# Sliding-window attention: products with the values for two query blocks at once, and one copy of both every second slot

## The chip, the cores and the metric

The kernel runs on one core of one Trainium2 chip. The metric is the device time of one execution in microseconds (us); lower is better. The engines are named as in the profile: PE is TensorE's matmul part, PEld its weight loads, DVE is VectorE, ACT is ScalarE, POOL is GpSimd, SP is SyncE, whose queue issues the transfers.

## What is computed

A block with 2048 tokens of width 512. The input is normalised, goes through attention with 32 heads of width 16 and a window of 256 keys, and through a gated feed-forward part of width 1792:

```python
xn = layernorm(x)                                   # 2048 x 512
q, k, v = split(xn @ wqkv)                          # 32 heads, 16 wide
scores = q @ k.T * 16 ** -0.5                       # per head
mask = (i - j >= 0) & (i - j < 256)
s = (softmax(where(mask, scores, -1e9)) @ v) @ wo
g = silu(gelu(layernorm(xn) @ w1 + b1) @ w2 + b2)
out = x + s * g                                     # all in float32
```

With blocks of 128 tokens, the window of a query block reaches over its own key block and the two before it.

## The kernel before

The program has one core's instructions in an order written by hand: a list of fillers and planned steps gives each step its slot, and all engines but SP keep that order. There are two long stages. Up to about 449 us attention runs, with the projections and a part of the feed-forward's first product as fillers; after that comes the rest of the feed-forward, the output projection and the gate.

Attention is cut into 128 slots: 8 groups of four heads (`n`) times 16 blocks of 128 tokens. Slot `t` does, in PE's order:

1. `prob_block(..., 1)`: scores of key block `t` against up to three query blocks (384 columns) for two of the four heads into the bank pair `stb`, in two matmuls side by side, one in the upper 64 rows of the array, one in the lower. ACT takes the exponential into `pt`, and POOL clears what lies outside the window in the first and the last 128 columns (`affine_select`).
2. `max_block`: for query block `t + 12` (`LEAD = 12`), the scores against the window's keys, to get the row maxima. The two newer key blocks go to `xy` (four matmuls of 256 columns), the oldest to `zo[:, :, 0:256]` (four of 128). DVE puts the part of `zo` that lies in the window into `xy` (`copy_predicated`) and takes the maximum (`tensor_reduce`). The maxima become an extra row of the queries through a small transfer, so that the exponential needs no separate subtraction.
3. `fill_in(t, 0)`: fillers, mostly projections of later heads into the banks `fb`. `tandem` runs two of them side by side on half the array's rows each; in the middle of their span (`mid`) the two banks change rows.
4. `prob_block(..., 0)`: as 1., for the other two heads; then `fill_in(t, 1)`.
5. `pv_step` for query block `t - 1`: the products with the values. `vt` holds the values with a column of ones (17 columns a head), so that the denominators come along. For each of the up to three key blocks and each of the four heads there is one product of 128 columns, with the head's 17 output rows at partition 32 times its number, so that the four heads' products lie side by side in the array's columns. They add up in `otb`, 128 columns of the bank `zo[:, 1]`, whose first 256 columns belong to `max_block`.
6. ACT copies `otb` to a quarter of `oraw`; every fourth slot SP sends `oraw` to memory (`oT_d`).

```python
otb = zo[:, 1, 256:384]
```

`xy`, `zo`, `stb` and `otb` exist once, so each is written again only after its readers are done. Readers and writers of one bank are kept apart by waits: the first `zo<-qk` matmul of `max_block` waits for ACT's copy of `otb`, and the first product of `pv_step` for DVE's `copy_predicated`. A plain float32 product is two matmuls in the instruction stream, which the counts of the profile show.

In the profile nearly all instructions carry line L42, that of a helper which issues them; they are told apart by their tiles: `zo<-pt,vt` the products with the values, `oraw<-zo` the copy, `zo<-qk` and `xy<-qk` the scores for the maxima, `stb<-qk` those for the exponential, `fb<-...` the fillers.

Of the kernel before, what the change touches and what calls it, by code (L numbers as in the profile page):

```python
# [9 lines left out]
F32 = mybir.dt.float32  # L10
# [7 lines left out]
S, D, H, DH, WIN, F = 2048, 512, 32, 16, 256, 1792  # L18
P = 128
# [30 lines left out]
def mixer_kernel(ctx, tc, x, wqk, wv, wo, w1, b1, w2, b2, out):  # L50


    nc = SimpleNamespace(**{name: Ordered(tc, name) for name in ("tensor", "vector", "scalar", "gpsimd", "sync")})
# [4 lines left out]
    small = ctx.enter_context(tc.tile_pool(name="small", bufs=3))  # L58
# [72 lines left out]
    def run(steps):  # L131
        for step in steps:
            step()
# [13 lines left out]
    def open_slot(i):  # L147
        slots.append(bigp.tile([P, 2, 2, S], F32R, tag=f"qk{i}", name=f"qk{i}"))
# [13 lines left out]

    xy = psum.tile([P, 2, 512], F32, name="xy")
    zo = psum.tile([P, 2, 512], F32, name="zo")
    otb = zo[:, 1, 256:384]
    fb = [psum.tile([P, 512], F32, name=f"fb{i}") for i in range(2)]
    early = ExitStack()
    ps_st = early.enter_context(tc.tile_pool(name="ps_st", bufs=2, space=PSUM))
# [8 lines left out]
    vt = vp.tile([P, NKB, 16, DH + 1], F32, name="vt")  # L177
# [210 lines left out]
    def pair_h(f):  # L388
# [11 lines left out]
                behind(t, nc.sync.dma_start, h_d[f - 6], raw)  # L400
        return 3 * KT, mm, finish

    def tandem(t0, t1, one, two, mid=None, back=None):

        n = one[0]
        lo, hi = slice(0, 64), slice(64, P)
        mid = mid or max(1, (t0 + t1 + 1) // 2)
        most = n // 4  # L410

        def places(slots, last):

            last = min(most, n // (len(slots) + 1)) if last else 0
            cuts = [(n - last) * k // len(slots) for k in range(len(slots) + 1)]
            out = []
            for t, a, b in zip(slots, cuts, cuts[1:]):
                ahead = min(b - a, max(most, (b - a + 1) // 2))
                out += [(t, 0)] * ahead + [(t, 1)] * (b - a - ahead)
            return out + [(t1, 0)] * last  # L420

        first, second = places(range(t0, mid), False), places(range(back or mid, t1), True)
        for phase, where in enumerate((first, second)):
            for i in range(n):
                flags = dict(start=(phase == 0 and i == 0), stop=(phase == 1 and i == n - 1), skip_group_check=True)
                def unit(i=i, phase=phase, flags=flags):
                    (two if phase == 0 else one)[1](fb[1 - phase], i, hi, **flags)
                    (one if phase == 0 else two)[1](fb[phase], i, lo, **flags)
                fills.setdefault(where[i], []).append((unit, ()))
        fills[t1, 0].append((one[2], (fb[0], t1, nc.scalar.copy)))  # L430
        fills[t1, 0].append((two[2], (fb[1], t1, nc.vector.tensor_copy)))
# [12 lines left out]

    mts = {}

    def max_block(n, qb):

        slot = slots[n % 2]
        if qb % 4 == 0:  # L450
            mts[n, qb // 4] = small.tile([P, 2, 2, 4], F32, tag="mt", name=f"mt_{n}_{qb}")
        lo = max(qb - 1, 0)
        off = 128 * (lo + 1 - qb)

        def scores(p, a, first):
            r = slice(64 * a, 64 * a + 64)
            out, keys = ((zo[:, a, P * p: P * (p + 1)], slice(P * (qb - 2), P * (qb - 1))) if first else
                         (xy[:, a, 256 * p + off: 256 * (p + 1)], slice(P * lo, P * (qb + 1))))
            nc.tensor.matmul(out, slot[r, 0, p, P * qb: P * (qb + 1)], slot[r, 1, p, keys], start=True, stop=True)

        for p, a, first in ((0, 1, False), (0, 0, False), (1, 1, False), (1, 0, False),
                            (0, 1, True), (0, 0, True), (1, 1, True), (1, 0, True)):
            if qb >= 2 or not first:
                scores(p, a, first)
        four = xy.rearrange("q a (p k) -> q a p k", p=2)
        nc.vector.copy_predicated(four[:, :, :, 128:256], mask,
                                  neg if qb < 2 else zo[:, :, 0:256].rearrange("q a (p k) -> q a p k", p=2))
        nc.vector.tensor_reduce(out=mts[n, qb // 4][:, :, :, qb % 4],
                                in_=four[:, :, :, off:256],
                                axis=AX.X, op=ALU.max, negate=True)  # L470
# [15 lines left out]
    pts = {}  # L486

    def prob_block(n, kb, p):
        slot = slots[n % 2]
        w = min(384, S - P * kb)  # L490
        pt = pp.tile([P, 2, 384], F32, tag="pt", name=f"pt_{n}_{kb}_{p}")
        both = xy if p and 16 * n + kb + LEAD >= 16 * NQ else stb[0]
        for a in (1, 0):
            r = slice(64 * a, 64 * a + 64)
            nc.tensor.matmul(both[:, a, 0:w], slot[r, 1, p, P * kb: P * (kb + 1)],
                             slot[r, 0, p, P * kb: P * kb + w], start=True, stop=True)
        nc.scalar.activation(pt[:, :, 0:w], both[:, :, 0:w], AF.Exp, scale=DH ** -0.5)
        nc.gpsimd.affine_select(out=pt[:, :, 0:P], in_=pt[:, :, 0:P], pattern=[[0, 2], [1, P]],
                                compare_op=ALU.is_ge, fill=0.0, base=0, channel_multiplier=-1)
        if w == 384:  # L500
            nc.gpsimd.affine_select(out=pt[:, :, 256:384], in_=pt[:, :, 256:384],
                                    pattern=[[0, 2], [-1, P]], compare_op=ALU.is_gt, fill=0.0,
                                    base=0, channel_multiplier=1)
        pts[(n, kb, p)] = pt


    outs = {}

    def pv_step(n, qb):

        lo = max(qb - 2, 0)
        for kb in range(lo, qb + 1):
            for j in range(4):
                nc.tensor.matmul(otb[32 * j: 32 * j + DH + 1], vt[:, kb, (4 * n + j) % 16],
                                 pts[n, kb, j // 2][:, j % 2, P * (qb - kb): P * (qb - kb + 1)],
                                 start=(kb == lo), stop=(kb == qb),
                                 skip_group_check=True, tile_position=(0, 32 * j))
        if qb % 4 == 0:
            outs[0] = sgp.tile([P, 512], F32, tag="or", name=f"oraw_{n}_{qb}", bufs=2)
        nc.scalar.copy(outs[0][:, P * (qb % 4): P * (qb % 4 + 1)], otb)  # L520
        if qb % 4 == 3:
            (at if n or qb > 7 else behind)(16 * n + qb + 2, nc.sync.dma_start, oT_d[n // 2, n % 2::2, :, P * (qb - 3): P * (qb + 1)], outs[0])

# [81 lines left out]
    def at(t, fn, *args):  # L605
        plan.setdefault(t, []).append((fn, args))
# [33 lines left out]
    n, raw = raws["qk"]  # L640
# [27 lines left out]
    for place, todo in spread([job_qk(1, 0), job_qk(1, 1)], [(t, k) for t in range(-2, 3) for k in range(2)]).items():  # L668
        fills.setdefault(place, []).extend(todo)
    soon = {}  # L670
    tandem(3, 8, pair_qk(1, 2), pair_qk(1, 3))
    for n, spans in enumerate((((9, 14), (15, 19)), ((20, 24), (25, 30)), ((31, 35), (36, 41)), ((42, 47), (48, 53, 51)),
                               ((75, 79), (80, 84)), ((85, 90), (93, 98))), 2):
# [68 lines left out]
    def fill_in(t, half):  # L742
        now[:] = t, half
        run(delayed.pop((t, half), ()))
        for fn, args in fills.get((t, half), ()):
            fn(*args)

    end = 16 * NQ
    for t in range(-16, end + 1):
        m = t + LEAD  # L750
        if t == -5:
            open_slot(1)
            for k in range(4):
                at(-4 + k, clear_part, k)
        if 0 <= t < end:
            if t == 0:
                early.close()
                stb.append(attn.enter_context(tc.tile_pool(name="ps_s2", bufs=1, space=PSUM)).tile(
                    [P, 2, 512], F32, name="stb"))
            prob_block(t // 16, t % 16, 1)  # L760
        if t >= 0 and m < end:
            max_block(m // 16, m % 16)
        fill_in(t, 0)
        for fn, args in plan.get(t, []):
            fn(*args)
        if 4 <= m < LEAD:
            max_block(0, m)
        if 0 <= t < end:
            prob_block(t // 16, t % 16, 0)
        fill_in(t, 1)  # L770
        if 0 <= m < 4:
            max_block(0, m)
        if t >= 1:
            pv_step((t - 1) // 16, (t - 1) % 16)
        run(lns.get(t, ()))
        if 0 <= m < end and m % 4 == 3:
            max_rows(m // 16, m % 16 // 4, t)
        for fn, args in ends.get(t, []):
            fn(*args)
# [20 lines left out]
    for f in range(6, NF, 2):  # L800
        t = gp.tile([P, 2, 512], F32, tag="ohl", name=f"hr_{f}", bufs=4)
# [403 lines left out]
```

## Time and profile before

| | us |
|---|---|
| median of 3 runs | 773.82 |
| lowest and highest of them | 773.26, 775.31 |
| the profiled execution, its own time | 776.17 |
| its span, first to last instruction | 774.5 |

| engine | busy us | share | instructions |
|---|---|---|---|
| PE | 747.9 | 97% | 7428 |
| PEld | 583.5 | 75% | 7428 |
| DVE | 533.4 | 69% | 865 |
| ACT | 435.3 | 56% | 724 |
| POOL | 281.5 | 36% | 567 |

The granted TensorE clock is 0.998 of full speed over the span. A matmul's length in the profile includes its way through the array, so matmuls that overlap fill PE's row, and a PE that is busy 97% of the time isn't at its peak: what a stretch of matmuls costs is read from the starts of one and of the next. The chain of work that ended last is followed back from the last instruction; an engine's share of it is time that it alone held up the end, as far as the profile shows. A releaser named in a wait is the one that came last.

### The profile page before, as it was taken

To read this page: it belongs to the slowest core of one execution; us is meant where nothing else is said; L and a number is where in the kernel's file an instruction comes from. 1 tells how busy PE (TensorE), PEld (TensorE's weight loads), DVE (VectorE), ACT (ScalarE), POOL (GpSimd) and SP (SyncE) were. 2 spreads that over 40 slices of the span, in tenths; PEclk is the share of its full clock that TensorE was granted. 3 is DMA by queue.
4 is the path that set the end of the run, shared out by engine and by line. 5 is a ranking of instruction groups with operands and counts; after the bars stand their busy time and mean duration, and the time that the engine had idled before them with its cause. 6 is when DMAs were issued, how large, how long until landed. Compare 5 with 4: busy or idle time off the path is not lost.

```text
span 774.5 us, 18774 instructions
## 1 busy us (share of the span) xinstructions
PE 747.9 (97%) x7428; PEld 583.5 (75%) x7428; DVE 533.4 (69%) x865; ACT 435.3 (56%) x724; POOL 281.5 (36%) x567
## 2 busy tenths in 40 slices
PE   9889999999999999999999999999999999999997
PEld 8777666676768887676676678888778778888886
DVE  7886777777777778887874447763657475676473
ACT  5536776767676666777877755444544444442001
POOL 6111666757565554766766800030101100000102
PEclk9999999999999999999999999999999999999999
DMA  7612445655446863455744283541102213243531
GB/s 258 204 44 52 106 110 121 172 114 139 111 92 201 256 213 98 107 150 138 186 128 151 61 287 118 180 150 56 68 28 98 92 61 101 84 137 135 177 96 54
DMA packets 56951, 99.40 MB, mean 128 GB/s; under 512 B 11104, under 2 KB 11360, under 8 KB 56864
## 3 DMA queue, kind: packets, MB, share of 16 engines
q1 hardware_dynamic: 56864, 98.21, 43.4%
q8 instruction: 58, 0.95, 0.5%
q14 instruction: 29, 0.24, 0.1%
HBM read 51.39 MB, written 29.62 MB: 105 GB/s over the span
## 4 chain that ended last, share of the span: by engine, by line
PE 80%; DVE 9%; ACT 6%; issue 3%; POOL 2%; DMA 1%; SPq 0%; DVEq 0%; ACTq 0%; POOLq 0%
PE acc L42 18%; PE fb L42 17%; PE zo L42 13%; PE stb L42 8%; PE p L42 7%; PE s L42 6%; PE xy L42 5%; PE h L42 5%; ACT pt L42 3%; PE pv L42 1%; DVE xnT L42 1%; DVE xy L42 1%; DVE mt L42 1%; POOL pt L42 1%; DVE bnA L42 1%
## 5 line engine op out<-in xcount | busy, mean ns | idle before, releaser
L42 POOL TENSOR_SCALAR_AFFINE_SELECT pt<-pt 128x256 f32<-128x256 f32 x480 | 193.6, 428 | 158.8 <-ACT pt L42 156.5
L42 ACT ACTIVATE pt<-stb 128x768 f32<-128x768 f32 (+1 forms) x244 | 188.7, 773 | 55.3 <-PE stb L42 46.2
L42 DVE TENSOR_REDUCE mt<-xy 128x4 f32<-128x1024 f32 (+1 forms) x128 | 152.6, 1192 | 4.4
L42 PE MATMUL acc<-w,gh 128*128 128x512 f32 x432 | 133.3, 390 | 0.0
L42 DVE COPY_PREDICATED xy<-upper,zo 128x512 f32<-128x512 int32 x112 | 77.5, 692 | 69.4 <-PE zo L42 67.5
L42 PE MATMUL fb<-xnT,wqb 64*128 64x512 f32 (+1 forms) x684 | 115.4, 405 | 0.5 <-DVE xnT L42 0.5
L42 PE MATMUL zo<-pt,vt 128*17 128x128 f32 x2880 | 103.9, 275 | 2.2 <-DVE xy L42 1.6
L42 PE MATMUL stb<-qk 64*128 64x384 f32 (+1 forms) x488 | 96.6, 391 | 7.2 <-ACT pt L42 5.8
L42 POOL TENSOR_TENSOR xo<-xo,gated 128x512 f32<-128x512 f32 x15 | 20.2, 1350 | 220.9 <-DVE gated L42 217.3
L42 PEld LDWEIGHTS zo<-pt,vt 128*17 128x17 f32 x2880 | 67.4, 97 | 39.7 <-issue 18.0
L42 PEld LDWEIGHTS acc<-w,gh 128*128 128x128 f32 x432 | 80.8, 188 | 16.6
L42 PEld LDWEIGHTS stb<-qk 64*128 64x128 f32 x488 | 45.5, 183 | 52.1 <-ACT pt L42 41.0
L42 PE MATMUL acc<-w,gl 128*128 128x512 f32 x216 | 84.2, 390 | 0.0
L42 PEld LDWEIGHTS fb<-xnT,wqb 64*128 64x128 f32 (+1 forms) x684 | 63.4, 186 | 7.3 <-DVE xnT L42 0.6
L42 PE MATMUL xy<-qk 64*128 64x256 f32 (+2 forms) x536 | 61.7, 304 | 5.5 <-DVE mt L42 4.7
L42 ACT COPY oraw<-zo 128x128 f32<-128x128 f32 x128 | 34.2, 267 | 40.5 <-PE zo L42 36.4
L42 PEld LDWEIGHTS xy<-qk 64*128 64x128 f32 x536 | 43.8, 185 | 17.2 <-DVE mt L42 9.8
L42 PEld LDWEIGHTS acc<-w,gl 128*128 128x128 f32 x216 | 40.5, 188 | 8.7 <-DVE gl L42 0.3
L42 ACT ACTIVATE gated<-acc 128x512 f32<-128x512 f32 x16 | 8.7, 596 | 64.0 <-DVE acc L42 64.0
L42 PE MATMUL s<-wos,ohl 128*128 128x512 f32 (+1 forms) x204 | 44.7, 377 | 0.0
L42 DVE TENSOR_TENSOR gl<-g,gh 128x512 fp32r<-128x512 f32 x38 | 28.1, 740 | 20.6 <-ACT gh L42 19.3
L42 PEld LDWEIGHTS s<-wos,ohl 128*128 128x128 f32 x204 | 36.6, 188 | 7.0
(182 smaller groups left out, 1172.3 us busy)
## 6 DMA issues: line engine op xcount, KB each, us to landing
qk<-sh SPq DMA_DIRECT2D x128, 128.0 KB
qk<-pjr SPq DMA_DIRECT2D x64, 128.0 KB
oT_d<-oraw SPq DMA_DIRECT2D x32, 256.0 KB
w_d<-in_w_dram SPq DMA_DIRECT2D x14, 512.0 KB
x<-in_x_dram SPq DMA_DIRECT2D x16, 256.0 KB
or<-oT_d SPq DMA_DIRECT2D x16, 256.0 KB
w<-rden_d SPq DMA_DIRECT2D x16, 256.0 KB
xo<-in_x_dram SPq DMA_DIRECT2D x16, 256.0 KB
```

The source lines that it names most:

```text
L42: r = issue(*args, **kwargs)
```

## The change

`pv_step` now works on pairs of query blocks. `otb` is 256 columns, both blocks of a pair. In the slot of the even block the two key blocks before the pair are taken: the newer of them for both query blocks in one product of 256 columns, the older for the even block alone, 128 columns. In the slot of the odd block come the pair's own two key blocks: the even one for both query blocks (256 columns), the odd one for the odd block (128). A slot has 8 products in place of 12, with the same number of columns in all. The sums stay open in `otb` from the even slot to the odd one, and ACT copies 256 columns after the odd block.

Two things go with it. `max_block`'s `zo<-qk` matmuls of the bank with `otb` come between the two halves of an open sum; there they no longer carry the flag that marks the whole bank as fresh (`amid`). And where a slot with an even block comes just before the middle of a `tandem`, ACT reads one column of `otb` (`seen`), so that the order of the work around that middle stays fixed by a wait, as it was by the copy; there are 14 of these.

```diff
-    otb = zo[:, 1, 256:384]
+    otb = zo[:, 1, 256:512]
...
+    turns = set()
...
         mid = mid or max(1, (t0 + t1 + 1) // 2)
+        turns.add(mid - 1)
...
-    def max_block(n, qb):
+    def max_block(n, qb, amid=False):
...
-            nc.tensor.matmul(out, slot[r, 0, p, P * qb: P * (qb + 1)], slot[r, 1, p, keys], start=True, stop=True)
+            nc.tensor.matmul(out, slot[r, 0, p, P * qb: P * (qb + 1)], slot[r, 1, p, keys],
+                             start=not (amid and first and a), stop=True, skip_group_check=amid)
...
     def pv_step(n, qb):
 
-        lo = max(qb - 2, 0)
-        for kb in range(lo, qb + 1):
+
+        even = qb - qb % 2
+        blocks = ((1,) if qb else (0,)) if even == 0 else (even, qb) if qb % 2 else (even - 1, even - 2)
+        for kb in blocks:
+            first, last = max(even, kb), min(even + 1, kb + 2)
             for j in range(4):
-                nc.tensor.matmul(otb[32 * j: 32 * j + DH + 1], vt[:, kb, (4 * n + j) % 16],
-                                 pts[n, kb, j // 2][:, j % 2, P * (qb - kb): P * (qb - kb + 1)],
-                                 start=(kb == lo), stop=(kb == qb),
+                nc.tensor.matmul(otb[32 * j: 32 * j + DH + 1, P * (first - even): P * (last + 1 - even)],
+                                 vt[:, kb, (4 * n + j) % 16],
+                                 pts[n, kb, j // 2][:, j % 2, P * (first - kb): P * (last + 1 - kb)],
+                                 start=(kb == max(even - 1, 0)), stop=(kb >= even),
                                  skip_group_check=True, tile_position=(0, 32 * j))
-        if qb % 4 == 0:
+        if qb % 2 == 0:
+            if 16 * n + qb + 1 in turns:
+                nc.scalar.copy(small.tile([P, 1], F32, tag="seen", name=f"seen_{n}_{qb}"), otb[:, 0:1])
+            return
+        if qb % 4 == 1:
             outs[0] = sgp.tile([P, 512], F32, tag="or", name=f"oraw_{n}_{qb}", bufs=2)
-        nc.scalar.copy(outs[0][:, P * (qb % 4): P * (qb % 4 + 1)], otb)
+        nc.scalar.copy(outs[0][:, 128 * (qb % 4 - 1): 128 * (qb % 4 + 1)], otb)
...
-            max_block(m // 16, m % 16)
+            max_block(m // 16, m % 16, t >= 2 and t % 2 == 0)
```

## The prediction

> **What bounds the kernel now.** I read first the page's busy time and the chain of work that ended last, then the stages.
>
> ```profile
> span 774.5 us, 18774 instructions
> PE 747.9 (97%) x7428; PEld 583.5 (75%) x7428; DVE 533.4 (69%) x865; ACT 435.3 (56%) x724; POOL 281.5 (36%) x567
> ...
> PE 80%; DVE 9%; ACT 6%; issue 3%; POOL 2%; DMA 1%; SPq 0%; DVEq 0%; ACTq 0%; POOLq 0%
> PE acc L42 18%; PE fb L42 17%; PE zo L42 13%; PE stb L42 8%; PE p L42 7%; PE s L42 6%; PE xy L42 5%; PE h L42 5%; ACT pt L42 3%; PE pv L42 1%; DVE xnT L42 1%; DVE xy L42 1%; DVE mt L42 1%; POOL pt L42 1%; DVE bnA L42 1%
> ```
>
> TensorE (PE) is busy 97% and holds 80% of the chain; zo, where the values' products land, has 13% of it. The change touches only the slots. The first values' product starts at 77.7 us, the last score block for the maxima is done near 418, the last copy of the values at 449.3, so I cut there in the view by stretches of time (columns: stretch, length, busy us and instructions of each engine).
>
> ```profile
> 77.70:418.00 340.30, 330.16 (x5055) 241.88 (x5054) 264.29 (x364) 242.28 (x418) 215.03 (x467) 1.00 0.54 143
> 418.00:449.30 31.30, 30.80 (x469) 21.82 (x468) 12.04 (x22) 23.91 (x42) 20.63 (x46) 1.00 0.39 118
> 449.30:774.50 325.20, 316.88 (x1422) 260.32 (x1422) 196.25 (x354) 126.70 (x210) 26.38 (x20) 1.00 0.34 111
> ```
>
> In the first stretch PE is busy 330 of 340 us, ScalarE (ACT) 242. What the change takes off ACT is thus worth nothing by itself; what it does to PE's order of work counts. The last 325 us don't change.
>
> The groups by form, for what is removed:
>
> ```profile
> L42 PE MATMUL zo<-pt,vt 128*17 128x128 f32 x2880 | 103.9, 275 | 2.2 <-DVE xy L42 1.6
> L42 PEld LDWEIGHTS zo<-pt,vt 128*17 128x17 f32 x2880 | 67.4, 97 | 39.7 <-issue 18.0 <-DVE xy L42 16.7 <-POOL pt L42 1.5
> ...
> L42 ACT COPY oraw<-zo 128x128 f32<-128x128 f32 x128 | 34.2, 267 | 40.5 <-PE zo L42 36.4 <-DVE mt L42 2.8 <-DMA w_d<-in_w_dram 0.3
> ...
> L42 ACT COPY pjr<-fb 128x512 f32<-128x512 f32 x15 | 8.8, 586 | 6.1 <-PE fb L42 4.4 <-PE stb L42 1.7
> ```
>
> Then one slot in order of time (start, length, operation):
>
> ```profile
> 300.70 0.45 PE L42 MATMUL stb<-qk 64*128 64x384 f32 x2
> 300.81 0.37 PEld L42 LDWEIGHTS xy<-qk 64*128 64x128 f32 x4
> 300.84 0.27 ACT L42 COPY oraw<-zo 128x128 f32<-128x128 f32 x1 [0.69 <-PE zo L42]
> 300.99 0.40 PE L42 MATMUL xy<-qk 64*128 64x256 f32 x4
> ...
> 301.16 0.30 PEld L42 LDWEIGHTS zo<-qk 64*128 64x128 f32 x4
> 301.22 0.38 PE L42 MATMUL zo<-qk 64*128 64x128 f32 x4
> 301.27 0.81 ACT L42 ACTIVATE pt<-stb 128x768 f32<-128x768 f32 x1 [0.16 <-PE stb L42]
> ...
> 301.44 0.91 PE L42 MATMUL fb<-xnT,wqb 64*128 64x512 f32 x6
> ...
> 302.18 0.40 PE L42 MATMUL stb<-qk 64*128 64x384 f32 x2
> ...
> 302.42 0.39 PE L42 MATMUL fb<-xnT,wqb 64*128 64x512 f32 x2
> ...
> 302.63 0.81 ACT L42 ACTIVATE pt<-stb 128x768 f32<-128x768 f32 x1 [0.54 <-PE stb L42]
> ...
> 302.74 0.85 PE L42 MATMUL zo<-pt,vt 128*17 128x128 f32 x24
> ...
> 303.52 0.38 PE L42 MATMUL stb<-qk 64*128 64x256 f32 x2
> ```
>
> A slot lasts 2.8 us (300.70 to 303.52) and the values' 24 matmuls take 0.78 of it (302.74 to 303.52). The copy of the values runs at the start of the next slot, 300.84 to 301.11. The weight load of zo<-qk, the oldest block's scores for the maxima, starts at 301.16, 0.05 after it. The built program has a wait of that load for ACT in 100 of 112 places (zo and the values share a bank).
>
> **The change, part by part.**
>
> *Fewer, longer products.* A logical product is two matmuls. 1440 become 960, 2880 matmuls 1920; an even slot and an odd slot each stream 256+128 columns per head in place of three times 128. The columns are the same, so only what a matmul costs beside its columns is saved.
>
> ```profile
> 124.31 0.40 PE L42 MATMUL fb<-xnT,wqb 64*128 64x512 f32 x2
> ...
> 124.63 0.30 PE L42 MATMUL zo<-pt,vt 128*17 128x128 f32 x4
> ```
>
> Four heads run side by side: the first four of this block last 0.30, one alone 0.275, so they start within 0.025. In the block of 24 above, 0.85 less 0.275 leaves 0.575 between the first and the last start; less that 0.025, 0.55 for five rounds of four, 0.11 a round. Is any of it not columns? Pairs of xy<-qk (256 columns) go by in 0.115 (300.99 to 301.22, two pairs), pairs of fb (512 columns) in 0.25 (301.44 to 302.18, three): proportional, with no fixed part. I take 3 ns a round, hardly more than zero: 720 rounds become 480, 240 x 0.003 = -0.7 us. Ends: 0, and -6.0 if every round paid the 0.025 of its starts.
>
> The Trainium skill has a rule here: TensorEngine Tiling, Instruction Overhead, gives every matmul about 60 cycles beside its columns. By an estimate from that figure and the 2.4 GHz in the Trainium skill's TensorE: Matmul & The Clock Gate, What's actually happening, 240 rounds would give back 240 x 25 ns = 6.0 us; by that rule the sum below would be 5.3 us lower, and the pairs of 256 and 512 columns speak against it.
>
> *One copy every second slot.* From 128 columns in 267 ns to 512 in 586, a column is 0.83 ns, so 256 take 0.373: 64 such copies are 23.9 us, and the 14 new one-column copies at 0.16 make 2.2, against 34.2: ACT saves 8 us. Off the path: in the slot above the exponential starts at 301.27, 0.12 after its scores' end at 301.15, and a copy that ended at 301.22 would still be ahead of it.
>
> What is on the path is the load of zo<-qk behind the copy. After an odd block it waits 0.107 longer, and behind it on PE stand the fillers, the second score block and the values. After an even block it waits for nothing or for a one-column copy. Both prices need to know where that load is the last:
>
> ```profile
> 81.30 0.27 ACT L42 COPY oraw<-zo 128x128 f32<-128x128 f32 x1
> ...
> 81.61 0.30 PEld L42 LDWEIGHTS zo<-qk 64*128 64x128 f32 x4
> ...
> 293.97 0.27 ACT L42 COPY oraw<-zo 128x128 f32<-128x128 f32 x1
> ...
> 294.13 0.44 PE L42 MATMUL stb<-qk 64*128 64x384 f32 x2 [0.39 <-ACT pt L42]
> ...
> 294.65 0.34 PE L42 MATMUL zo<-qk 64*128 64x128 f32 x4
> ...
> 294.83 0.44 PE L42 MATMUL fb<-xnT,wqb 64*128 64x512 f32 x2
> ...
> 409.13 0.27 ACT L42 COPY oraw<-zo 128x128 f32<-128x128 f32 x1 [0.69 <-PE zo L42]
> ...
> 409.44 0.30 PEld L42 LDWEIGHTS zo<-qk 64*128 64x128 f32 x4
> ```
>
> The first and last after an odd block start 0.04 after the copy ends. I read all 100 such pairs: the load is held by the copy in 33 of 50 after an odd block and 33 of 50 after an even one. Where the copy was long done, as at 293.97, zo<-qk to the fillers takes 294.65 to 294.83, 0.18; where it holds, 301.22 to 301.44, 0.22. So an even place gives 0.04 (six of them 0.1): -1.7 us. An odd place is already held, so it takes the 0.107 in full, a few of the 33 less: +3.2. Ends: nothing given back, and 50 odd places, +5.4.
>
> In four of the odd places the next slot waits for an exponential held up by a cast that asks nothing of PE, and the delay is lost in that wait: -0.4.
>
> *A second wait ahead of the values.* In the built program the block's first load waits for VectorE (DVE) alone in 93 slots; after the change for DVE and GpSimd (POOL), which costs an instruction more on PE's queue. Cover: PE drains when it changes its tiling. The block at 124.63 had two waits before and starts 0.32 after its filler (124.31), as the one with a single wait does (302.42 to 302.74). Where the cover ends:
>
> ```profile
> 107.40 0.19 PEld L42 LDWEIGHTS stb<-qk 64*128 64x128 f32 x2 [0.21 <-ACT pt L42]
> ...
> 107.65 0.33 PEld L42 LDWEIGHTS xy<-qk 64*128 64x128 f32 x4
> ...
> 317.35 0.67 DVE L42 COPY_PREDICATED xy<-upper,zo 128x512 f32<-128x512 int32 x1
> ...
> 318.08 0.24 PEld L42 LDWEIGHTS zo<-pt,vt 128*17 128x17 f32 x12 [0.95 <-DVE xy L42]
> ```
>
> Where DVE is last, as at 318.02, the cover is gone: there are 16 such starts, 0.06 behind DVE's end. Price of a wait instruction: at 107.40 two of them stand between two loads 0.25 apart that without them are 0.11 apart (300.70, 300.81), so 0.07 each. 16 x 0.075 = +1.2; ends 0 and, in all 93, +7.0.
>
> *Fewer waits on ACT.* 98 exponentials had two or three waits, 56 have; with them one starts 0.12 after its scores (301.15 to 301.27), without 0.05 (302.58 to 302.63). PE asks for that only where it waits for ACT, the second line of this list of waits (us in total, times, longest):
>
> ```profile
> PEld xy L42 <- DVE mt L42: 9.8, 20, 1.7
> ...
> PE stb L42 <- ACT pt L42: 5.8, 15, 1.0
> ```
>
> Half of 15 places, 0.08 each, cut to -0.3; ends 0 and, if half of that wait went, -2.9.
>
> *At no cost.* The larger clearing of zo (once, while x is still loading; below the 0.27 of a copy of as many columns if that cover were gone), the flag that leaves the bank's marks, the order of key blocks (an odd slot's newest block is still second to last by time, 0.43 in place of 0.44 into the block; an even one no longer needs it), the stores of the values (issued 0.107 later, read after 449).
>
> Sum: -0.7 + 3.2 - 1.7 - 0.4 + 1.2 - 0.3 = +1.3 us. The profiled execution took 776.17 (774.5 of span), 2.35 over the median of 773.82, so 777.5 there and 775.1 in the median, +0.17%. A difference below 0.3%, 2.3 us, counts as none.
>
> **The rivals.**
>
> *The gain of the even slots is not had* (chance 0.20). The load of xy waits for DVE's maximum in 20 places, 9.8 us (first line of the waits); where DVE decides, zo<-qk 0.04 earlier helps only if DVE's copy starts earlier too. Without the 1.7 and the absorbed 0.4: +3.4, 777.2, slower. It decides once DVE's ring and not PE sets the slot; for it speaks DVE's 264 us in the stretch, against it PE's 330.
>
> *The second wait ahead of the values isn't covered* (0.13): 93 x 0.075 = 7.0 in place of 1.2, so 780.9, slower. It decides once DVE ends less than some 0.13 us (0.06 and the 0.07 of a wait) before most blocks start. For it speaks the load's wait for DVE (16.7 us in the group above), against it the start at 124.63.
>
> *ACT's relief reaches PE* (0.14). The 8 us off ACT shorten the late exponentials, half of the 5.8 goes, and PE's waits soak up half of the 3.2: 775.1 - 2.6 - 1.6 = 770.9, faster. Against it: in a late slot, as at 294.13, PE comes with the scores after the copy began, and the copy ends (294.24) before the scores do (294.57).
>
> *Time goes by the matmul, not the column* (0.03): 16 in place of 24 would take a third of 0.575, 0.19 in each of 120 slots, 23 us in place of 0.7: 773.8 + 1.3 + 0.7 - 23 = 753. Against it pairs of 512 columns that take twice those of 256. The Trainium skill's Instruction Overhead points this way, by less.
>
> That the products aren't wider is excluded: the built program has 960 of them, half of 256 columns.
>
> **How the numbers follow.** My forecast, no difference beyond 0.3%, has 0.50, its own range 771.5 to 776.1. Slower: 0.20+0.13 = 0.33. Faster: 0.14+0.03 = 0.17. The predicted time is 775.1. The range runs from 770.9, ACT's relief, to 779.5, most of the uncovered wait; outside are the 753 and part of 780.9 and of the rivals' tails.
>
> **What would show it.** Right: values' blocks last as long as before for both slots (0.78 to the next stb), the copy near 0.37, zo<-qk to fillers some 0.1 later after odd blocks and 0.04 shorter after even ones, 340 us of the first stretch within 2. Wrong: a block that shrinks with its count of matmuls; a start of the values more than 0.33 after the filler in many slots; PE's wait for ACT falling from 5.8 to under 3.

## The result: 0.56% slower, and the loss lies where no changed line is at work

The changed kernel takes 779.54 us (median of 6 runs, 777.50 to 780.35) against 774.57 (773.26 to 776.72) for the kernel before in the same session: a ratio of 1.0056, 95% interval 1.0034 to 1.0078 (ratios here and below are taken over all executions and are not quotients of the two medians, which would be 1.0064 here). The profiled execution took 780.27, with a span of 778.6. Executions of one kernel differ by up to 3.5 us, and the traces show 2.5 of it ahead of the slots (the first product with the values starts at 77.74 us in the kernel before and at 75.25 in the experiment e3 below), so stages are compared by their own lengths.

The head of the page of the changed kernel, then its view by stretches of time, cut where the same work begins and ends (its last copy of the values starts 0.55 us earlier):

```profile
span 778.6 us, 16794 instructions
PE 753.0 (97%) x6468; PEld 560.6 (72%) x6468; DVE 532.5 (68%) x865; ACT 426.7 (55%) x674; POOL 280.8 (36%) x567
77.70:418.00 340.30, 330.59 (x4201) 221.44 (x4202) 263.49 (x365) 234.30 (x373) 214.99 (x467) 1.00 0.55 143
418.00:448.75 30.75, 30.48 (x363) 18.92 (x362) 11.56 (x21) 23.16 (x38) 20.16 (x45) 1.00 0.38 116
448.75:778.60 329.85, 321.99 (x1422) 260.89 (x1422) 196.62 (x354) 126.77 (x210) 26.28 (x20) 1.00 0.35 110
```

TensorE executes 960 matmuls fewer and is busy 5.1 us longer (747.9 to 753.0). In the slots nothing is lost; the last stretch, where no line of the diff is at work, goes from 325.2 us to 329.85 with the same 1422 matmuls. That is the whole loss. Where in it? The groups by form, first of the kernel before, then of the changed one:

```profile
L42 PE MATMUL acc<-w,gh 128*128 128x512 f32 x432 | 133.3, 390 | 0.0
L42 PE MATMUL acc<-w,gl 128*128 128x512 f32 x216 | 84.2, 390 | 0.0
L42 PE MATMUL s<-wos,ohl 128*128 128x512 f32 x180 | 41.8, 390 | 0.0
L42 PE MATMUL h<-xnT 128*128 128x512 f32 x112 | 32.3, 389 | 0.0
L42 PEld LDWEIGHTS acc<-w,gh 128*128 128x128 f32 x432 | 80.8, 188 | 16.6
```

```profile
L42 PE MATMUL acc<-w,gh 128*128 128x512 f32 x432 | 136.5, 397 | 0.0
L42 PE MATMUL acc<-w,gl 128*128 128x512 f32 x216 | 85.6, 396 | 0.0
L42 PE MATMUL s<-wos,ohl 128*128 128x512 f32 x180 | 41.9, 391 | 0.0
L42 PE MATMUL h<-xnT 128*128 128x512 f32 x112 | 32.4, 390 | 0.0
L42 PEld LDWEIGHTS acc<-w,gh 128*128 128x128 f32 x432 | 81.0, 188 | 19.2
```

Only acc, the second product of the feed-forward part (`project`), is clearly slower (s and h by 1 ns): 397 ns in place of 390, with no idle time before it and with loads of the same 188 ns. From one start to the next the median goes from 227 to 234 ns, in every chunk and with the granted clock at 1.00: 648 x 7 ns = 4.5 us. The timelines show it as three matmuls in 0.68 us before (first fence, gl to gl) and 0.71 after:

```profile
467.02 0.39 PE L42 MATMUL acc<-w,gl 128*128 128x512 f32 x1
467.25 0.62 PE L42 MATMUL acc<-w,gh 128*128 128x512 f32 x2
467.70 0.39 PE L42 MATMUL acc<-w,gl 128*128 128x512 f32 x1
```

```profile
466.56 0.40 PE L42 MATMUL acc<-w,gl 128*128 128x512 f32 x1
466.80 0.63 PE L42 MATMUL acc<-w,gh 128*128 128x512 f32 x2
467.27 0.40 PE L42 MATMUL acc<-w,gl 128*128 128x512 f32 x1
```

One group of the changed kernel was spared. The first 24 matmuls of acc load their weights from g_first, not from gh and gl:

```profile
L42 PE MATMUL acc<-w,g_first 128*128 128x512 f32 x24 | 5.7, 395 | 0.7 <-ACT hf L42 0.7
453.29 4.48 PE L42 MATMUL acc<-w,g_first 128*128 128x512 f32 x19
```

19 of them in 4.48 us: less the last one's 0.39, 18 steps of 227 ns. Same operation, same moving w2, same chunk; only the tile that the weights come from differs. g_first lies in the pool bigp. In the built program gh and gl lie in a pool that stands behind the pool small, and the diff gives small one more tag, `seen`: three buffers of one column, each rounded up to 32 bytes a partition. So everything behind it lies 96 bytes higher: gh from byte 193280 (755 x 256) to 193376. w2, at 83200 (325 x 256), and g_first stay.

### The profile page after: what moved, and what is told of

Same layout as the page of the kernel before. It is cut to its first block, busy times and chain, and to the rows that moved or that the text cites. A ratio compares the mean times of both kernels' runs of the same rounds, so it can differ in the third digit from the quotient of the medians.

```text
span 778.6 us, 16794 instructions
## 1 busy us (share of the span) xinstructions
PE 753.0 (97%) x6468; PEld 560.6 (72%) x6468; DVE 532.5 (68%) x865; ACT 426.7 (55%) x674; POOL 280.8 (36%) x567
## 4 chain that ended last, share of the span: by engine, by line
PE 82%; DVE 8%; ACT 5%; issue 2%; POOL 2%; DVEq 0%; ACTq 0%
PE acc L42 19%; PE fb L42 17%; PE zo L42 13%; PE stb L42 8%; PE p L42 7%; PE h L42 6%; PE s L42 6%; PE xy L42 5%; ACT pt L42 3%; POOL pt L42 2%; DVE xy L42 1%; PE pv L42 1%; DVE mt L42 1%; DVE xnT L42 1%; DVE bnA L42 1%
## 5 line engine op out<-in xcount | busy, mean ns | idle before, releaser
L42 PE MATMUL acc<-w,gh 128*128 128x512 f32 x432 | 136.5, 397 | 0.0
L42 PE MATMUL zo<-pt,vt 128*17 128x128 f32 (+1 forms) x1920 | 103.1, 329 | 2.6 <-DVE xy L42 1.1
L42 PEld LDWEIGHTS zo<-pt,vt 128*17 128x17 f32 x1920 | 44.1, 96 | 61.1 <-issue 20.6
L42 PE MATMUL zo<-qk 64*128 64x128 f32 x448 | 40.6, 258 | 0.0
```

Source lines behind the costliest of these rows:

```text
L42: r = issue(*args, **kwargs)
```

## The experiments

**Is it the placement? (e1)** The kernel before, plus nothing but the tag:

```diff
     def pv_step(n, qb):
+        if n == qb == 0:
+            small.tile([P, 1], F32, tag="seen", name="pad")
         lo = max(qb - 2, 0)
```

> The kernel before, with one thing of the change alone: the tag 'seen' in the pool small is opened (three buffers of 32 bytes a partition, never written or read), so that every tile of a pool behind it, gh and gl among them, lies 96 bytes higher, as in the changed kernel; no instruction is added or moved. Placement theory (a load of gh or gl that lies 96 bytes off the moving w2 disturbs the product that runs beside it): acc goes from 227 to 234 ns a matmul, 648 x 7 ns = 4.5 us, so ratio 1.006 (778.5 to 780) and the attention stage as before within 0.5 us. Rival, the loss comes from the changed order of the values (what they leave behind on the queues or in the clock): 1.000, acc at 227.

778.87 us against 775.62, ratio 1.0050 (1.0036 to 1.0064). Not one instruction is added, and acc has the changed kernel's rows to the digit:

```profile
L42 PE MATMUL acc<-w,gh 128*128 128x512 f32 x432 | 136.5, 397 | 0.0
L42 PE MATMUL acc<-w,gl 128*128 128x512 f32 x216 | 85.6, 396 | 0.0
```

From the first to the last start of a values' block this kernel takes 370.12 us, the kernel before 370.61. The loss is one of placement; the rival, the order of the values, is out.

**The address of gh and gl, or their distance from w2? (e2)** The kernel before with 96 bytes ahead of everything:

```diff
+    const.tile([P, 24], F32, name="pad")
     ident = const.tile([P, P], F32, name="ident")
```

> The kernel before with 96 unused bytes ahead of the very first constant, so that every tile of the kernel's own, w2 and gh and gl alike, lies 96 bytes higher and no two of them stand otherwise to each other. If what counts is the distance between the loaded and the moving operand: acc at 227, ratio 1.000. If what counts is the address of the loaded operand by itself: acc at 234, and h, p and s as well perhaps, ratio 1.006 or more.

775.67, ratio 0.9996 (0.9986 to 1.0007). gh and gl lie at the very addresses of the changed kernel, and w2 96 bytes higher too:

```profile
L42 PE MATMUL acc<-w,gh 128*128 128x512 f32 x432 | 133.3, 390 | 0.0
L42 PE MATMUL acc<-w,gl 128*128 128x512 f32 x216 | 84.2, 390 | 0.0
```

So the address of the loaded operand by itself doesn't count; the distance between loaded and moving operand does.

**Does it hold for another pair? (e4)** s<-wos,ohl had been spared, since both its tiles moved by the same 96. Here only wos, its moving operand, is moved, in the kernel before:

```diff
+    cp.tile([P, 24], F32, name="pad")
     wos = cp.tile([P, 2, 4, 512], F32R, name="wos")
```

> The kernel before with 96 unused bytes ahead of wos alone. gh, gl, w2 and ohl stay. Distance theory: acc at 227, but s<-wos,ohl, which lay at 227 in both kernels, goes to 234 (204 matmuls x 7 ns = 1.4 us, ratio 1.0018). If it is something of gh and gl or of their pool alone: s at 227, ratio 1.000.

```profile
L42 PE MATMUL s<-wos,ohl 128*128 128x512 f32 x180 | 43.0, 396 | 0.0
L42 PE MATMUL acc<-w,gh 128*128 128x512 f32 x432 | 133.4, 390 | 0.0
```

s goes from 226.8 to 233.6 ns a step (390 to 396 in the group), acc stays. The time, 776.00, ratio 1.001 (1.0000 to 1.0020), agrees with the 1.4 us that this makes, though its interval starts at no change: the rows decide here, not the time.

**The change without the displacement (e3, e10).** First the one-column copies go into a tag that exists:

```diff
-  nc.scalar.copy(small.tile([P, 1], F32, tag="seen", name=f"seen_{n}_{qb}"), otb[:, 0:1])
+  nc.scalar.copy(small.tile([P, 1], F32, tag="ve1", name=f"seen_{n}_{qb}"), otb[:, 0:1])
```

> The changed kernel, with the 14 one-column copies written to the existing tag ve1 in place of a tag of their own; all tiles then lie where they lay before. Placement theory: acc back at 227 ns, the 4.5 us gone, and what the change does to the attention stage is left: 0.5 us faster than before, ratio 0.999 (773.5 to 774.5). Rival, order of the values: ratio stays at 1.006 and acc at 234. The sum of the prediction, +1.3, gives 1.0017.

775.10, ratio 0.9992 (0.9983 to 1.0002); acc back at 227. Then the tag stays, with buffers of 256 bytes, which displaces all behind it by 768:

```diff
-  nc.scalar.copy(small.tile([P, 1], F32, tag="seen", name=f"seen_{n}_{qb}"), otb[:, 0:1])
+  nc.scalar.copy(small.tile([P, 64], F32, tag="seen", name=f"seen_{n}_{qb}")[:, 0:1], otb[:, 0:1])
```

> The changed kernel with one number changed: the buffers of the tag 'seen' are 256 bytes a partition each in place of 4 (rounded up to 32), so that all behind it lies 768 bytes higher than before, and not 96. If only the distance within 256 bytes counts: acc and s at 227, ratio as with the tag ve1, 0.998 to 1.000. If any displacement of gh and gl from where they lay disturbs: 1.005.

```profile
L42 PE MATMUL acc<-w,gh 128*128 128x512 f32 x432 | 133.3, 390 | 0.0
L42 PE MATMUL acc<-w,gl 128*128 128x512 f32 x216 | 84.2, 390 | 0.0
```

775.25, ratio 0.9997 (0.9984 to 1.0010). A number in one allocation, 1 column or 64, decides 0.5% of the kernel. What the change itself is worth is thus no difference that these runs can tell.

**Which distances disturb? (e7, e8)** The kernel before with unused bytes ahead of gh, gl and wos, so that one run tries three distances. One diff for both; e7 has 8, 8 and 32 columns of 4 bytes, e8 32, 8 and 16 (each pad also moves what stands behind it):

```diff
+    cp.tile([P, 32], F32, name="pad")
     wos = cp.tile([P, 2, 4, 512], F32R, name="wos")
...
+        if not pads:
+            gp.tile([P, 8], F32, tag="pa", name="pa", bufs=1)
         gh = gp.tile([P, 512], F32R, tag="gh", name=f"gh_{c}_{f}")
+        if not pads:
+            gp.tile([P, 8], F32, tag="pb", name="pb", bufs=1)
+        pads.append(1)
         gl = gp.tile([P, 512], F32R, tag="gl", name=f"gl_{c}_{f}")
```

> The kernel before with unused bytes ahead of gh (32), of gl (32 more, so 64) and of wos (192 in all); w2 and ohl stay. Any distance that is no multiple of 256 bytes disturbs: acc before gh, acc before gl and s all near 234 ns a matmul. A rule by 64 bytes: only gh (32) is disturbed, gl (64) and s (192) stay at 227.

> As the run with 32, 64 and 192 bytes, with 128 ahead of gh, 160 of gl and 224 of wos. A rule by 128 bytes: gh at 227, gl (32 over 128) and s (32 short of 256) at 234. A rule by 256 bytes: all three at 234. A rule by 64: as by 128 here.

One execution each, 779.75 and 780.60; acc and s:

```profile
L42 PE MATMUL acc<-w,gh 128*128 128x512 f32 x432 | 135.2, 394 | 0.0
L42 PE MATMUL s<-wos,ohl 128*128 128x512 f32 x180 | 43.0, 395 | 0.0
```

```profile
L42 PE MATMUL acc<-w,gh 128*128 128x512 f32 x432 | 136.1, 396 | 0.0
L42 PE MATMUL s<-wos,ohl 128*128 128x512 f32 x180 | 43.0, 396 | 0.0
```

By the matmul beside which the displaced tile is loaded (mean, start to next start; 226.4 to 227.3 undisturbed): gh behind gh at 32 bytes 230.4, at 128 230.1; gl at 64 232.6, at 160 236.8; s with wos at 192 and at 224 233.3 both. No rule by 64 or by 128 bytes: of the distances tried only multiples of 256 were free, the others cost 3 to 10 ns a matmul in these rows.

How the price depends on the distance stays open, and the distance isn't all of it. With gh at 128, the step from gl to gh takes 233.5 where that from gh to gh takes 230.1, with the same moving tile: the place in the sequence counts too. And with wos at 224 the loaded tile lies 32 behind the moving one modulo 256, as with gh at 32, yet the steps take 233.3 and 230.4. Nor is it shown that only the load beside a matmul counts. A matmul of h, whose own tiles are not displaced, takes 228.4 (96 bytes, changed kernel), 235.0 (32, e7) and 232.6 (128, e8) in place of 226.8 when a displaced gh is loaded beside it (ten steps each). But a matmul of acc with displaced weights, beside which a tile of h is loaded that is not displaced, takes 230.3, 239.0 and 229.4 in place of 226.6 as well (seven steps each). So part of the disturbance reaches steps whose next load isn't displaced.

**Is the hold at the odd places on the path? (e6, e5, e9)** All three start from e3. In e6 the copy of the values is made in two, so that it ends later:

```diff
-        nc.scalar.copy(outs[0][:, 128 * (qb % 4 - 1): 128 * (qb % 4 + 1)], otb)
+        for h in range(2):
+            nc.scalar.copy(outs[0][:, 128 * (qb % 4 - 1 + h): 128 * (qb % 4 + h)], otb[:, 128 * h: 128 * h + 128])
```

> The changed kernel with tiles where they lay before, and the copy of 256 columns made as two of 128 (2 x 0.267 in place of 0.373), so that the load of zo<-qk is held 0.16 longer after every odd block. If each held place is on the path: 33 x 0.16 = +5.3 us, ratio about 1.006 beside the 0.9992 of the kernel it is made from. If such delays are lost in later waits: +2 or less, ratio 1.002 at most.

776.86, ratio 1.0023 (1.0012 to 1.0035). I had the size wrong: two copies overlap, and take 0.43 together where one takes 0.37:

```profile
301.96 0.43 ACT L42 COPY oraw<-zo 128x128 f32<-128x128 f32 x2 [0.68 <-PE zo L42]
```

So the load is held 0.06 longer, not 0.16. The odd places grow by 0.034 on average, 50 x 0.034 = 1.7 us, and the values from first to last start by 1.46 (370.05 to 371.51): most of a longer hold does reach the end. That gives the price of a longer hold, not that a shorter one would be a gain. For that e5 issues a pair of fillers ahead of the held load, in 41 places:

```diff
+            if first and ahead:
+                ahead[0][0](*ahead.pop(0)[1])
             if qb >= 2 or not first:
                 scores(p, a, first)
...
-            max_block(m // 16, m % 16, t >= 2 and t % 2 == 0)
+            todo = fills.get((t, 0), [])
+            ahead = [todo.pop(0)] if t > 2 and t % 2 and t - 1 not in turns and m % 16 > 1 and todo and todo[0][0].__name__ == "unit" else []
+            max_block(m // 16, m % 16, t >= 2 and t % 2 == 0, ahead)
```

> The changed kernel with tiles where they lay before (the 14 one-column copies in ve1), and in 41 of the slots that follow an odd block one pair of fb matmuls (0.25 us) is issued between the scores of xy and those of zo, so that the load of zo<-qk no longer stands waiting for the copy of 256 columns. If that wait is on the path, as the prediction priced it (0.107 longer, +3.2 in 33 places): some 0.1 us less in each held place, 3 to 4 us, ratio 0.994 to 0.996. If the time is given back further on, since zo now ends 0.12 later for VectorE: ratio 0.998 to 1.001.

778.60, ratio 1.0044 (1.0027 to 1.0061): both expectations missed, the cover costs. zo comes 0.21 later after the second pair of xy (0.147 to 0.358 on average), and VectorE, which needs zo, and then xy, which needs VectorE's maximum, come later with it. The list of waits, of e3 and of e5:

```profile
PEld xy L42 <- DVE mt L42: 10.1, 22, 1.7
```

```profile
PEld xy L42 <- DVE mt L42: 13.2, 36, 1.7
```

22 such waits become 36, and the values take 373.45 us in place of 370.05. In e9 the values lie in the other bank of zo:

```diff
-    otb = zo[:, 1, 256:512]
+    otb = zo[:, 0, 256:512]
...
-                             start=not (amid and first and a), stop=True, skip_group_check=amid)
+                             start=not (amid and first and not a), stop=True, skip_group_check=amid)
```

> The changed kernel with tiles where they lay before, and the 256 columns of the values in the other bank of zo (that of a=0 in place of a=1). The first of the two side-by-side zo products (a=1) then has no bank in common with the copy; only the second waits for it. If a held place costs by the wait at its load: the load of a=1 goes ahead, some 0.05 of the 0.1 is covered in each of 33 odd places, 1 to 2 us, ratio 0.997 to 0.998. If the end of zo, for which VectorE waits, is what decides: it comes as late as before, ratio 0.999.

775.34, ratio 1.0003 (0.9992 to 1.0013). It tells the two theories apart no further: the first load of zo<-qk is held in 29 of 50 odd places as in e3, so the wait hangs on the tile zo, not on the bank, and nothing had been taken away.

No version was faster than the kernel before by a difference that could be measured; e3 came nearest.

## Why the prediction was right or wrong

The predicted time was 775.1 with no difference as the likeliest case; it came out slower, 779.54, 0.04 past the end of the range (779.5), and for the reason of none of the rivals. By the ratio it is 773.82 x 1.0056 = 778.2 on the base from which the prediction started, inside the range; that is luck, since this end was priced for waits that aren't covered, and those did not come.

**The step that failed** is "The last 325 us don't change." I went by the instructions, of which none in that stretch changes, and didn't ask where their operands lie. The same hole is in "At no cost": the one-column copies do cost ScalarE no more than priced (14 of 159 ns), but they needed a place, and that moved gh and gl. It is worth +4.5 us; without it (e3, e10) the kernel is within 0.1% of the one before, as the likeliest case had it.

**The terms within the slots**, from the traces of four kernels with the old values and three with the new, slot by slot (the same slot agrees to about 5 ns among kernels of one kind):

- *Fewer, longer products*, -0.7: a block goes from 0.780 to 0.775, over 127 blocks -0.6. Two rounds fewer a block are worth 5 ns, so 2.5 a round. The 25 a round that the prediction estimated from the 60 cycles of the Trainium skill's TensorEngine Tiling (Array Packing), Instruction Overhead, did not come.
- *Odd places*, +3.2: from the second pair of xy to the fillers, the 50 places grow by 3.16 us in all. The sum is right, its split isn't: 26 places grow by 0.07 or more, 0.12 on average, where the prediction had 33 of some 0.1. The -0.4 for delays that a later wait takes up was not looked for by itself.
- *Even places*, -1.7: they shrink by 1.77.
- *A second wait ahead of the values*, +1.2: the count was right and the price a little low, but it is not on the path. In 16 starts VectorE is last; the first product came 0.054 after its end, and now, in the 15 where it is still last, 0.147: 0.092 each. But those 16 slots are then shorter, by a median of 0.09. The slot that the prediction shows for it, in the changed kernel:

```profile
317.72 0.68 DVE L42 COPY_PREDICATED xy<-upper,zo 128x512 f32<-128x512 int32 x1
318.43 1.23 DVE L42 TENSOR_REDUCE mt<-xy 128x4 f32<-128x1024 f32 x1
318.52 0.16 PEld L42 LDWEIGHTS zo<-pt,vt 128*17 128x17 f32 x8 [0.63 <-POOL pt L42]
319.71 0.19 PEld L42 LDWEIGHTS xy<-qk 64*128 64x128 f32 x2 [0.59 <-DVE mt L42]
```

and in the kernel before:

```profile
318.06 1.23 DVE L42 TENSOR_REDUCE mt<-xy 128x4 f32<-128x1024 f32 x1
319.34 0.30 PEld L42 LDWEIGHTS xy<-qk 64*128 64x128 f32 x4 [0.51 <-DVE mt L42]
```

The first load of the values comes 0.12 after VectorE's copy ends (318.40), where that of before (318.08) came 0.06 after the end at 318.02. (The row names POOL, the other of the two waits; its clearing ended at 318.37, 0.03 before VectorE's copy.) But the next scores, xy, wait for VectorE's maximum in both: 1.31 and 1.32 after that copy. Whatever lies between is free; in 14 of the 16 slots of the kernel before, xy starts 0.05 after that maximum. I had asked what is last at the start of the values, and not what is last after it, though the list of waits showed 20 such waits for the maximum.

- *Fewer waits on ACT*, -0.3: TensorE's wait for the exponentials fell from 5.8 to 5.0 us. The relief of ScalarE by 8.6 us (435.3 to 426.7) brought no more, as the forecast had it against its rival.

The 100 slots with a load of zo<-qk make +0.7 together. The other 27, among them those with no such load and the last ones, are 1.0 us shorter, which I had not forecast and have not split further. From first to last start the values' stage goes from 370.33 (mean of four) to 369.98 (mean of three): -0.35 where the sum said +1.3.

**The rivals.** The second wait hardly spread beyond the starts that I counted: in the changed kernel 18 lie 0.15 behind VectorE's copy. Time by the matmul, the 753, is out: a block lost 5 ns and not 0.19 us. "It decides once DVE's ring and not PE sets the slot" was the sentence nearest to what e5 and the 16 starts show: in part of the slots that ring does set the time.

## What to carry to other kernels

A new tile, however small and wherever used, can move every tile that is allocated behind it: compare the addresses of the operands of the busiest matmuls before and after a change, and try keeping the loaded and the moving operand a multiple of 256 bytes apart (round a new buffer up, or reuse an old one). That is shown here for 128x128 weights beside 512 moving columns alone. When a kernel slows in code that was not touched, look for a group whose mean duration changed with no idle time before it. And a delay is priced only when the next wait behind it is known: 0.09 at each of 16 starts was worth nothing, because the engine that was late anyway was asked again right after.

## What the runs showed of the hardware that I had not expected

In long rows of matmuls with a weight load beside each, a matmul takes 3 to 10 ns more than 227 when the loaded and the moving tile are not a multiple of 256 bytes apart within a partition, in all the cases tried (loaded tile displaced by 32, 64, 96, 128 or 160 bytes, moving tile by 96, 192 or 224). Moving both by 96 made no odds (e2), and the load itself keeps its 188 ns. The Trainium skill says otherwise: in TensorE: Matmul & The Clock Gate, Step-by-step: what each phase is for, TensorE has two independent read ports into SBUF, and "Loading the next tile's weights doesn't steal SBUF read bandwidth from the running matmul." At distances of a multiple of 256 bytes the traces agree, at the others they don't (227 to 234 in e1, with no instruction changed). That the two reads meet in the memory is how I read it; no run shows the memory itself, and none took the loads away.

Two copies of 128 columns on ScalarE, one behind the other, took 0.43 us and not twice 0.267 (e6): the second starts 0.16 after the first.
